# Metered background matmuls and unread filler matmuls in a four-layer attention kernel

## The chip, the core and the metric

The kernel runs on one core of a Trainium2 chip. The metric is the device time of one execution in microseconds (us); the time before is 2522.28 us, the median of six runs (2517.03 to 2527.03). The engines are named as in the profile: PE is the matrix engine (its weight loads stand apart as PEld), ACT the scalar engine, DVE the vector engine, POOL and SP the other two; SP only issues DMA transfers here. "PEclk" is the share of full speed that PE's clock was granted.

## What is computed

Four layers act on x (2048 tokens, 640 features, 32 heads of 20). Layers 0 and 2 see a sliding window of 256 keys (weights A), layers 1 and 3 see all 2048 keys (weights B).

```python
def layer(x, wqkv, wo, mask):            # mask: 0 <= i - j < 256 in layers 0 and 2, none in 1 and 3
    q, k, v = heads(layernorm(x) @ wqkv)  # 32 heads of 20
    p = softmax(where(mask, q @ k.T * 20 ** -0.5, -1e9))
    return x + join(p @ v) @ wo
x = layer(x, A...); x = layer(x, B...); x = layer(x, A...); x = layer(x, B...)
```

## The kernel before

**Units and tiles.** A unit is one layer `l`, one chunk `c` of 512 queries and one group `g` of four heads. A full-attention unit has 64 score blocks of 128 keys by 512 queries (16 key blocks for each of four heads), a windowed one has 12. The main loop (L759 to L851) takes the blocks of all units in one list, three to a *tile* (two in some early tiles), 1657 tiles in all, one a tick. In each tick it emits, in this order for PE:

1. the score matmuls of tile `t` (QK, L790) into one of two PSUM sets of three banks; heads lie in different row groups of PE and so run beside each other;
2. the exponential of the tile on ACT (L804), which reads the set and writes `pt`;
3. background work, by `pump` (called at L812);
4. the value matmuls (PV, L843) of the oldest four finished blocks, two or three tiles back, and the end of a unit when there is one.

Two PSUM sets mean that QK of tile `t` must wait for the exponential of tile `t-2`, and the exponential of tile `t` for that QK.

**Background work.** Everything that is not attention proper is a generator: layer norm and transposes (`t_ln`, L341), values (`t_v`, L382), queries and keys (`t_qk_window` L441, `t_qk_full` L455, both by `project`, L314), the normalisation of a finished unit (`t_tail`, L685) and the output projection (`t_out`, L474). Each accumulates in PSUM bank 6, the only background bank once `end_early` (L227) has given up bank 5; `drop_m` (L223) frees it for the next tick, after an evacuation by DVE (L266; by ACT in layer 0, L264).

A projection is five accumulating matmuls of 512 columns (L318). Between them the generator yields `("hold", 0.22)`, in `t_v` and `t_out` `("hold", 0.14)`; `advance` (L177) then notes the task as *held*, and `choose` (L191) gives back a held task before it looks at anything else.

```python
def choose(blocked, limit=1 << 30):
    if state["held"] is not None:
        return state["held"]
```

`pump(credit)` (L203) adds to a running credit, capped at 1.0, and advances tasks until `choose` gives none; it calls `choose(state["credit"] <= 0.0)`, and a blocked choice gives only held tasks and tails. Tasks wait in `todo` in the order of the unit that needs them first.

**Forced work.** When a unit starts, `start_unit` (L633) calls `require` (L233) for the keys, queries and values it needs. If they are not ready, `require` advances tasks there and then, ahead of the tile's QK in PE's order. For full attention, queries, keys and values go out to DRAM (`k_d`, `q_d` at L464, `v_d` at L426) and are loaded per unit by `load_unit` (vt L599, kt L606, qt L608). `load_ahead` does that early, at most one unit a tick, as soon as the unit's data are written; if it has not by the unit's start, `ensure_loaded(u, True)` does it then. A `project` sends its result to DRAM, and its task counts as ready, only when the task is advanced once more after its last matmul. Weights come by `take_w` (L292), which loads the next projection's weights ahead (L285) where it knows it, and otherwise waits four ticks.

All DMAs are issued in program order on SP's queue.

Of the kernel before, what the change touches and what calls it, by code (L numbers as in the profile page):

```python
# [31 lines left out]
def kernel(  # L32
# [10 lines left out]
    nc = tc.nc  # L43
# [37 lines left out]
    ident = big.tile([P, P], BF16, name="ident", tag="ident")  # L81
# [3 lines left out]
    masks = big.tile([P, 3, C], BF16, name="masks", tag="masks")  # L85

    ps = psp.tile([P, 8, C], F32, name="ps", tag="ps")
# [64 lines left out]
    state = {"tick": 0, "held": None, "credit": 0.0, "early": True, "act": True, "unit": 0}  # L152
# [15 lines left out]
    def push(name, gen, need):  # L168
        insort(todo, Task(name, gen, need))
# [7 lines left out]
    def advance(task):  # L177
        state["running"] = task
        try:
            kind, n = next(task.gen)  # L180
        except StopIteration:
            drop(task)
            state["held"] = None
            return 0.0
        state["held"] = task if kind == "hold" else None
        if kind == "wait":
            task.wake = state["tick"] + n
            return 0.0
        return n
# [4 lines that stand above are left out]
        for t in tails:  # L194
            if t.wake <= state["tick"]:
                return t
        if not blocked:
            for t in todo:
                if t.wake <= state["tick"] and (t.need <= limit or t.holds):
                    return t  # L200
        return None

    def pump(credit):  # L203
        state["credit"] = min(state["credit"] + credit, 1.0)
        while True:
            t = choose(state["credit"] <= 0.0)
            if t is None:
                break
            state["credit"] -= advance(t)


    mfree = {5: (0, 0), 6: (0, 1)}
# [291 lines left out]
    def push_layer(l, c):  # L504

        need = [first_use(l, c, g) for g in range(G)]
        push(("ln", l, c), t_ln(l, c), need[0])
        if l == 1:
            push(("v", l, c, 0), t_v(l, c, (0,)), need[0])
            push(("v", l, c, 1), t_v(l, c, (1,)), need[4])  # L510
        else:
            push(("v", l, c), t_v(l, c, (0, 1)), need[0])
        for g in range(G):
            key = ("qk", l, c, g)
            if l % 2:
                push_proj(key, l, 1, g, t_qk_full(key, l, c, g), need[g])
            else:
                push_proj(
                    key, l, 0, g, t_qk_window(key, l, c, g), need[g], first=(l == 0 and c == 0)
                )  # L520


    class Unit:
        def __init__(self, l, c, g, part=None):
# [58 lines left out]
    index = {(u.l, u.c, u.g, u.part): n for n, u in enumerate(units)}  # L583
# [143 lines left out]
    def t_stats0(c):  # L727
        for i in range(4):
            stats(0, c, i)
            yield ("pe", 0.1)  # L730
        ready.add(("x", 0, c))
# [12 lines left out]
    with tc.manual_schedule():  # L744
        push("stats", t_stats0(0), 0)
        push_layer(0, 0)
        require(("xnT", 0, 0))
        other_constants()
        require(("qk", 0, 0, 0))

        def narrow(u):
            return u.l == 0 or (u.l, u.part) == (1, "a")

        banks = [b for u in units for b in u.banks]
        tiles = []
        n = 0
        while n < len(banks):
            size = 2 if len(tiles) % 2 and narrow(banks[n][0]) else 3
            tiles.append(banks[n : n + size])  # L759
            n += size  # L760

        started = set()
        pts = deque()
        pushed = set()
        for t in range(len(tiles) + 8):
            state["tick"] += 1
            n_b = 0
            if t < len(tiles):
                cur = tiles[t]
                n_b = len(cur)  # L770
                for b in cur:
                    u = b[0]
                    if id(u) not in started:
                        started.add(id(u))
                        if u.l == 0 and u.g == 0 and u.c + 1 < NC and u.c not in pushed:
                            pushed.add(u.c)
                            push(("stats", u.c + 1), t_stats0(u.c + 1), index[0, u.c + 1, 0, None])
                            push_layer(0, u.c + 1)
                            if u.c == 0:
                                push("prep_b", t_prep_b(), index[0, 1, G - 1, None])  # L780
                        state["unit"] = index[u.l, u.c, u.g, u.part]
                        state["act"] = u.l == 0
                        if state["early"] and not narrow(u):
                            end_early()
                        start_unit(u)
                sp = ps[:, 0:3, :] if t % 2 == 0 else ps[:, 3:6, :]
                for n in range(2):
                    for i, (u, j, m, b0, subs, first, last, end) in enumerate(cur):
                        for kc, q0, qn, col in subs[n : n + 1]:
                            nc.tensor.matmul(  # L790
                                sp[:, i, col * P : (col + qn) * P],
                                lhsT=u.k(kc, j), rhs=u.q(j, q0, qn), start=True, stop=True,
                            )
                for b in cur:
                    if b[-1]:
                        s_emitted(b[0])
                pt = ptp.tile([P, 3, C], BF16, name="pt", tag="pt")
                i = 0
                while i < n_b:
                    b0 = cur[i][3]  # L800
                    k = i
                    while k < n_b and cur[k][3] == b0:
                        k += 1
                    nc.scalar.activation(  # L804
                        out=pt[:, i:k, b0 * P :], in_=sp[:, i:k, b0 * P :],
                        func=ACT.Exp, scale=SCALE,
                    )
                    i = k
                for i, b in enumerate(cur):
                    pts.append((t, pt, i, b))  # L810
                load_ahead()
                pump(1.2 if cur[0][0].l == 0 else 0.6)  # L812
            else:
                pump(2.0)

            if 0 < t <= len(tiles):
                cur_, pt_ = masked
                i = 0
                while i < len(cur_):
                    m, b0 = cur_[i][2:4]  # L820
                    k = i
                    while k < len(cur_) and cur_[k][2] == m:
                        k += 1
                    if m is not None:
                        mv_ = masks[:, m, b0 * P :].unsqueeze(1).to_broadcast(
                            (P, k - i, C - b0 * P)
                        )
                        nc.vector.tensor_tensor(  # L828
                            out=pt_[:, i:k, b0 * P :], in0=pt_[:, i:k, b0 * P :], in1=mv_,
                            op=ALU.mult,  # L830
                        )
                    i = k
            if n_b:
                masked = (cur, pt)

            if len(pts) >= 4 and pts[3][0] <= t - (3 if pts[0][3][0].windowed else 2):
                group = [pts.popleft() for _ in range(4)]
                u, subs, end = group[0][3][0], group[0][3][4], group[3][3][7]
                first, last = group[0][3][5:7]
                for n, (kc, q0, qn, col) in enumerate(subs):  # L840
                    for _, pt, i, b in group:
                        j = b[1]
                        nc.tensor.matmul(  # L843
                            op[32 * j : 32 * j + VW, q0 * P : (q0 + qn) * P],
                            lhsT=u.v(kc, j), rhs=pt[:, i, col * P : (col + qn) * P],
                            start=(first and n == 0), stop=(last and n == len(subs) - 1),
                            skip_group_check=u.windowed,
                        )
                if end:
                    pv_emitted(u)  # L850
                    finish_unit(u)  # L851
        while tails or todo:
            state["tick"] += 1
            pump(5.0)


# [28 lines left out]
```

The softmax here doesn't subtract the row's maximum and nothing guards it: scores larger than these inputs give would overflow.

## Time and profile before

| | |
|---|---|
| median of six runs | 2522.28 us (2517.03 to 2527.03) |
| the profiled execution | 2518.07 us, its span 2516.4 us |
| mean granted PE clock | 0.739 |
| busy in the span | PE 2065.5, PEld 729.9, DVE 852.6, ACT 2264.0, POOL 48.2 us |
| L804 exponential, ACT | 1688 instructions, 2197.9 us busy |
| L790 QK of full attention, PE | 4096, 711.7 us busy |
| L843 PV of full attention, PE | 4096, 533.4 us busy |
| L318 projections, PE | 1280, 365.1 us busy |

The profile is one execution. "Busy" for PE is the union of matmuls whose ends are modelled. A group of instructions is given with its line, its engine, its operands and the idle time of the engine just ahead of it, with what ended it. In the timeline the columns are start, duration, engine, line, operation and count; a bracket at the end of a row is the engine's idle time before it and what released it.

### The profile page before, as it was taken

How to read it: one execution, taken by the hardware profiler on the slowest of the kernel's cores; microseconds unless marked ns; L12 is line 12 of the kernel's file. 1: busy time of each engine (PE TensorE's matmuls, PEld its weight loads, DVE VectorE, ACT ScalarE, POOL GpSimd, SP SyncE). 2: the span in 40 equal slices, each digit the busy share in tenths (PEclk: the TensorE clock that was granted, in tenths of full speed). 3: DMA queues.
4: the chain of work that ended last, by engine and by line, in shares of the span. 5: the costliest groups of instructions: out<-in, count | busy, mean ns of one | idle time of the engine just before them, and what ended most of it. 6: DMA issues, size and time to landing. Idle time of an engine off the chain costs nothing.

```text
span 2516.4 us, 37514 instructions
## 1 busy us (share of the span) xinstructions
PE 2065.5 (82%) x15424; PEld 729.9 (29%) x15424; DVE 852.6 (34%) x1925; ACT 2264.0 (90%) x1831; POOL 48.2 (2%) x113
## 2 busy tenths in 40 slices
PE   6889987887878888878887888888877787778777
PEld 3334432222322233223332233223322222222222
DVE  6686843321324343424343433643200010001001
ACT  6778856889998999999999988999999999999995
POOL 2000000000000000000000000000000000000000
PEclk9899989885866699757996589968755565556555
DMA  4212133332201043101221033104211010011000
GB/s 164 70 59 63 46 98 105 111 106 69 67 28 43 27 102 103 37 31 42 91 94 43 1 84 94 65 20 116 78 36 48 32 43 32 33 46 46 32 17 11
DMA packets 92892, 153.03 MB, mean 61 GB/s; under 512 B 8880, under 2 KB 59056, under 8 KB 92720
## 3 DMA queue, kind: packets, MB, share of 16 engines
q1 hardware_dynamic: 92720, 150.64, 19.1%
q8 instruction: 120, 1.97, 0.3%
q14 instruction: 52, 0.43, 0.1%
HBM read 120.46 MB, written 30.15 MB: 60 GB/s over the span
## 4 chain that ended last, share of the span: by engine, by line
ACT 47%; PE 29%; issue 13%; DVE 8%; DMA 2%; SPq 0%; ACTq 0%; POOL 0%; DVEq 0%
ACT pt L804 46%; PE ps L318 10%; PE ps L790 6%; PE ps L843 4%; PE ps L482 4%; PE ps L405 4%; DVE pt L828 2%; DMA wqk<-wqk_d 1%; DVE oT L668 1%; PE ps L369 1%; DVE st L266 1%; DVE qa L266 1%; DMA qt<-q_d 1%; DVE x_sb L490 1%; PE ps L714 0%
## 5 line engine op out<-in xcount | busy, mean ns | idle before, releaser
L804 ACT ACTIVATE pt<-ps 128x1536 bf16<-128x1536 f32 (+1 forms) x1688 | 2197.9, 1536 | 185.7 <-PE ps L790 168.8
L790 PE MATMUL ps<-qt,kt 32*128 32x512 bf16 x4096 | 711.7, 502 | 303.6 <-ACT pt L804 270.2
L843 PE MATMUL ps<-pt,vt 128*21 128x512 bf16 x4096 | 533.4, 507 | 5.5 <-DVE oT L668 4.3
L790 PEld LDWEIGHTS <-kt 32*128 32x128 bf16 x4096 | 204.2, 95 | 771.6 <-issue 738.6
L318 PE MATMUL ps<-xnT,wqk 128*128 128x512 bf16 x1280 | 365.1, 422 | 22.6 <-DMA wqk<-wqk_d 8.1
L828 DVE TENSOR_TENSOR pt<-pt,masks 128x1024 bf16<-128x1024 bf16 (+5 forms) x403 | 240.0, 625 | 215.7 <-ACT pt L804 215.4
L668 DVE CAST oT<-ps 128x512 bf16<-128x512 f32 x117 | 80.3, 686 | 505.5 <-PE ps L843 505.1
L843 PEld LDWEIGHTS <-vt 128*21 128x21 bf16 x4096 | 105.9, 91 | 330.4 <-issue 325.9
L482 PE MATMUL ps<-wop,on 128*128 128x320 bf16 x1024 | 177.3, 321 | 10.5 <-DVE x_sb L490 5.3
L318 PEld LDWEIGHTS <-wqk 128*128 128x128 bf16 x1280 | 116.7, 104 | 193.9 <-issue 105.0
L790 PE MATMUL ps<-qa,ka 32*128 32x384 bf16 (+2 forms) x1408 | 135.6, 324 | 31.0 <-ACT pt L804 28.6
L266 DVE CAST st<-ps 128x512 bf16<-128x512 f32 x119 | 82.3, 692 | 213.7 <-PE ps L318 212.4
L490 DVE TENSOR_TENSOR x_sb<-x_sb,ps 128x320 bf16<-128x320 bf16 x128 | 61.9, 484 | 184.6 <-PE ps L482 182.1
L482 PEld LDWEIGHTS <-on 128*128 128x128 bf16 x1024 | 97.3, 103 | 77.3 <-issue 37.8
L405 PE MATMUL ps<-wv,xnT 128*128 128x320 bf16 x640 | 112.1, 313 | 7.0 <-DVE vs L266 2.1
L718 DVE TENSOR_TENSOR on<-oT,ps 128x512 bf16<-128x512 bf16 x128 | 87.5, 684 | 86.9 <-PE ps L714 85.5
L843 PE MATMUL ps<-pt,va 128*21 128x384 bf16 (+2 forms) x1408 | 89.1, 322 | 18.3 <-DVE oT L668 17.7
L695 DVE RECIPROCAL rz<-ps 128x16 f32<-128x16 f32 x128 | 32.8, 256 | 156.2 <-PE ps L690 147.2
L790 PEld LDWEIGHTS <-ka 32*128 32x128 bf16 x1408 | 39.4, 96 | 118.4 <-issue 112.8
L405 PEld LDWEIGHTS <-xnT 128*128 128x128 bf16 x640 | 58.0, 100 | 49.5 <-issue 29.3
L714 PE MATMUL ps<-rT,spread 32*128 32x128 bf16 x512 | 63.7, 258 | 2.2 <-DVE rT L707 1.3
L369 PE MATMUL ps<-ident,xn 128*128 128x128 bf16 x320 | 35.5, 257 | 25.6 <-DVE xn L360 22.7
(50 smaller groups left out, 646.2 us busy)
## 6 DMA issues: line engine op xcount, KB each, us to landing
wqk<-wqk_d SPq DMA_DIRECT2D x120, 320.0 KB
kt<-k_d SPq DMA_DIRECT2D x53, 512.0 KB
vt<-v_d SPq DMA_DIRECT2D x53, 336.0 KB
qt<-q_d SPq DMA_DIRECT2D x75, 128.0 KB
k_d<-st SPq DMA_DIRECT2D x64, 128.0 KB
q_d<-st SPq DMA_DIRECT2D x64, 128.0 KB
v_d<-vs SPq DMA_DIRECT2D x16, 336.0 KB
wqk_d<-wqk SPq DMA_DIRECT2D x16, 320.0 KB
```

Source lines behind the costliest of these rows:

```text
L266: nc.vector.tensor_copy(out=out_, in_=in_)
L318: nc.tensor.matmul(pq, lhsT=wt[:, n, dc, :], rhs=xt[:, dc, :], start=(dc == 0), stop=(dc == KD - 1),)
L405: nc.tensor.matmul(pv, lhsT=xt[:, dc, i * P : (i + 1) * P], rhs=wv_sb[l % 2][:, dc, h * HD : (h + 1) * HD], start=(dc == 0), stop=(dc == K ...
L482: nc.tensor.matmul(yp, lhsT=on[:, g, qb * P : (qb + 1) * P], rhs=wop[:, g, i * HD : (i + 1) * HD], start=(g == 0), stop=(g == G - 1),)
L490: nc.vector.tensor_tensor(out=xv, in0=xv, in1=yp, op=ALU.add)
L668: nc.vector.tensor_copy(out=oT[:], in_=op)
L714: nc.tensor.matmul(zb[:, qb * P : (qb + 1) * P], lhsT=spread4[:, qb, :], rhs=rT[:], start=True, stop=True,)
L718: nc.vector.tensor_tensor(out=on[:, g, :], in0=oT[:], in1=zb, op=ALU.mult)
L790: nc.tensor.matmul(sp[:, i, col * P : (col + qn) * P], lhsT=u.k(kc, j), rhs=u.q(j, q0, qn), start=True, stop=True,)
L804: nc.scalar.activation(out=pt[:, i:k, b0 * P :], in_=sp[:, i:k, b0 * P :], func=ACT.Exp, scale=SCALE,)
L828: nc.vector.tensor_tensor(out=pt_[:, i:k, b0 * P :], in0=pt_[:, i:k, b0 * P :], in1=mv_, op=ALU.mult,)
L843: nc.tensor.matmul(op[32 * j : 32 * j + VW, q0 * P : (q0 + qn) * P], lhsT=u.v(kc, j), rhs=pt[:, i, col * P : (col + qn) * P], start=(first ...
```

## The change

`pump` takes its cap as a second argument. In layer 0 it stays 1.2 a tick with cap 1.0. In later layers a tick adds 0.56 instead of 0.6, and the cap is 0.6 instead of 1.0. After it, up to the start of unit (3, 1, 0), a new `keep_clock` emits matmuls of 512 columns into the free background bank, from two constant tiles; nothing reads them. It does so while no task is held, the credit is over 0.2 and the bank is free in this tick, and takes 0.22 of credit for each. The calls in the last eight ticks and in the closing loop get caps of 2.0 and 5.0.

```diff
-    def pump(credit):
-        state["credit"] = min(state["credit"] + credit, 1.0)
+    def pump(credit, most):
+        state["credit"] = min(state["credit"] + credit, most)
...
+    def keep_clock():
+
+        while state["held"] is None and state["credit"] > 0.2:
+            b = min(mfree, key=mfree.get)
+            if mfree[b][0] > state["tick"]:
+                return
+            nc.tensor.matmul(
+                ps[:, b, :], lhsT=ident[:], rhs=masks[:, 0, :], start=True, stop=True
+            )
+            state["credit"] -= 0.22
...
-                pump(1.2 if cur[0][0].l == 0 else 0.6)
+                if cur[0][0].l == 0:
+                    pump(1.2, 1.0)
+                else:
+                    pump(0.56, 0.6)
+                    if state["unit"] < index[3, 1, 0, None]:
+                        keep_clock()
             else:
-                pump(2.0)
+                pump(2.0, 2.0)
...
-            pump(5.0)
+            pump(5.0, 5.0)
```

## The prediction

> **What bounds the kernel now.** I read first the shares of the page, then stretches by stage, then the idle time of ACT, then the timeline around it. ACT is busy for 90% of the span. By stage it is the bound, but not always full:
>
> ```profile
> 500.00:1800.00 1300.00, 1088.70 (x8341) 388.60 (x8341) 482.94 (x1048) 1207.33 (x911) 14.56 (x40) 0.77 0.21 64
> ...
> 1900.00:2000.00 100.00, 77.68 (x476) 20.45 (x472) 6.60 (x18) 100.00 (x76) 0.00 (x0) 0.50 0.09 31
> ```
>
> The columns are window, length, busy us of PE, PEld, DVE, ACT and POOL, PEclk, DMA share, GB/s. In 1900 to 2000 there is no background work, PE runs at half clock, and ACT is full: half clock is enough for attention alone. From 500 to 1800 ACT is idle for 1300 - 1207.33 = 92.7 us. Over the span the exponential (L804) waits 168.8 us for QK, and that time is what the change can win. What such a wait looks like:
>
> ```profile
> 712.50 3.14 ACT L804 ACTIVATE pt<-ps 128x1152 bf16<-128x1152 f32 x5
> ...
> 714.38 2.31 PE L318 MATMUL ps<-xnT,wqk 128*128 128x512 bf16 x5
> 716.62 0.61 PE L843 MATMUL ps<-pt,va 128*21 128x384 bf16 x8
> ...
> 717.16 0.61 PE L790 MATMUL ps<-qa,ka 32*128 32x384 bf16 x6
> ...
> 717.88 2.47 ACT L804 ACTIVATE pt<-ps 128x1536 bf16<-128x1536 f32 x2 [2.25 <-PE ps L790]
> ```
>
> A projection, five matmuls in one piece, takes 2.24 us (714.38 to 716.62) at half clock after a quiet stretch, QK stands behind it, and ACT idles 2.25 us. At full clock the same piece lasts 1.25 us (first row of the next fence), and single pieces in every second tile cost nothing: 895 to 945 us has ACT busy 48.89 of 50 at PEclk 1.00. There is a second kind of wait, forced work at a unit's start:
>
> ```profile
> 1565.58 1.25 PE L318 MATMUL ps<-xnT,wqk 128*128 128x512 bf16 x5 [1.19 <-DMA wqk<-wqk_d]
> ...
> 1567.61 1.24 PE L318 MATMUL ps<-xnT,wqk 128*128 128x512 bf16 x5 [0.78 <-DVE qa L266]
> ...
> 1570.06 4.13 ACT L804 ACTIVATE pt<-ps 128x1536 bf16<-128x1536 f32 x3 [4.95 <-PE ps L790]
> ```
>
> ```profile
> 420.03 0.32 SPq L464 DMA_DIRECT2D q_d<-st  x1
> ...
> 421.36 0.43 SPq L608 DMA_DIRECT2D qt<-q_d  x1
> ...
> 423.60 0.61 PE L790 MATMUL ps<-qt,kt 32*128 32x512 bf16 x3 [4.33 <-DMA qt<-q_d]
> ...
> 424.34 1.45 ACT L804 ACTIVATE pt<-ps 128x1536 bf16<-128x1536 f32 x1 [4.43 <-PE ps L790]
> ```
>
> The first shows two forced projections, 2.03 us apart because the one background bank must be evacuated between them. The second shows a unit whose queries are stored and loaded back at its start: ACT idles 4.43 us. With two forced projections ahead of the same chain (432.95) the gap is 8.00 us, with one (1490.98) it is 6.13, and where the last projection lies two tiles back (449.63) it is 2.61.
>
> **What the diff does to the order.** I compared the order of PE's instructions in the two programs, tile by tile.
>
> *Metering does not split a projection.* The five matmuls of an accumulation are held, and a held task is advanced whatever the credit. So pieces of 2.24 us stay; what the new numbers change is how often a piece comes: 0.56 instead of 0.6 a tile, and no more than 0.6 saved up. Two adjacent pieces after "155" become one tile apart in the next pair. Background falls behind by up to four projections where it has a due time.
>
> *Fillers.* 444 are added, two each in 222 tiles without other background. 195 of these tiles lie in 17 stretches of 3 to 18 tiles, nearly all in the second half of a chunk of layer 1; layer 3 after 1807 us is nearly as before.
>
> *Forced work grows.* At the start of unit (1, 0, 0, b), 420 us, two projections where none was; at (3, 0, 0, a), 1490 us, two for one; at (2, 3, 0), 1565 us, six for two. And units (1, 0, 4), (1, 0, 5), (1, 0, 6), which were loaded 4, 6 and 7 tiles ahead, are now loaded at their start: the last projection stands one, one and two tiles before it, fillers in the tiles ahead of that.
>
> **Costs.**
> 1. (1, 0, 0, b): the gap of 4.43 becomes one like 432.95, 8.00: +3.6.
> 2. (1, 0, 4) to (1, 0, 6): two gaps like 4.43, one like 2.61, 11.5 together. After such a stall the clock has dropped, and the next piece has cost 1.04 to 1.36 (443.74, 459.91): three times 1.2 is 3.6. The double pieces at 524.91 and 555.92 (2.93 and 3.14 of gap) now lie inside these stalls and go. 11.5 + 3.6 - 6.1 = +9.0.
> 3. (3, 0, 0, a): 8.00 - 6.13 = +1.9.
> 4. (2, 3, 0): four more projections at 2.03: +8.1. Their weights took 4.08 us to land at 1561.45, the length of two projections, so I add nothing for them.
> 5. Fillers. No row has one, so bounds: nothing, where PE is at full clock (QK to next start 0.33, two at 0.216, PV about 0.3: 1.1 of ACT's 1.36 us a tile); at half clock, QK 0.54 to the next start, two at 0.45, PV 0.54 in three tiles of four: 1.84 us against 1.36. The rise takes about 5 us (the pieces from 2035.96 on: 2.25, 1.89, then 1.25). In 5 us PE does 2.7 tiles and ACT could do 3.7; one tile late, less the 0.75 by which QK is ahead, leaves about 0.4 (1.2 if nothing is ahead). 17 stretches: +6.8, bounds 0 and 20.
>
> The fillers wait for nothing new: the bank's evacuation was emitted at least a tick earlier, and DVE's 0.69 us copy is over. The next user of the bank is PE itself. DMA and POOL get no new work. The end, from the last exponential, has the same PE order.
>
> **Gains.** I listed each gap of the timeline over 0.4 us with the order of the changed program ahead of it.
> - A. First piece after a filler stretch: 715.63, 756.90, 799.57, 1047.53, 1096.37, 1338.93, 1381.69: 2.25 + 1.66 + 2.19 + 1.41 + 1.34 + 1.41 + 1.41 = 11.7. At full clock one piece costs about nothing: 11.0.
> - B. The piece after that, behind three tiles of a unit's tail (722.21, the rest at 756.90, 806.08, 1089.54, 1345.83, 1388.58): 2.06 + 2.58 + 2.33 + 1.1 + 2.07 + 1.22 = 11.4. Two adjacent pieces cost 1.29 even at full clock (1054.42), and the three tail tiles hold little PE work. At full clock a tile without background has about 0.4 of 1.36 us of matmul streaming, and after the pieces from 2035.96 on such tiles lose the clock within some 5 us: PEclk is 1.00 in 2056 to 2061 and 0.51 in 2061 to 2071. I take it to drop in half of the cases: 5.0.
> - C. Pieces behind tails with one filler tile, and transposes after the stretches (1150.78, 1440.95, 1474.56, 1704.16 and the like, 13.2 in all): 2.7.
> - D. The split doubles, nine of about 0.3; and the 5.14 gap at 383.14, a weight load that now has a tile more: 1.3 less. 3.8 (bounds 2 and 6).
>
> **Sum.** Costs 3.6 + 9.0 + 1.9 + 8.1 + 6.8 = 29.4; gains 11.0 + 5.0 + 2.7 + 3.8 = 22.5; net +6.9. Against the profiled execution's 2518.07 that is 2525; the median of the runs stands 4.2 above it, so 2529. Layer 0 and the last 700 us stay.
>
> [...]
>
> **Rivals.**
> - *Faster: the clock holds through the tail tiles.* Then B gives 7.5 (each down to its value at full clock, 1.29 or 0), C 7.2, and few stretches start at half clock (2 instead of 6.8): gains 11.7 + 7.5 + 7.2 + 3.8 = 30.2, costs 24.6, net -5.6: 2517, and 2510 if the three late loads cost half, as in the next case. It decides from the point where the tiles between stretches keep PEclk at 1.0. For: 2046 to 2056, clock 1.00 with light tiles among the pieces. Against: the drop at 2061.
> - *Same: the late loads cost half.* SP runs ahead of the other engines and may issue them sooner than their place says. Then cost 2 is 5.8 + 2.4 - 6.1 = 2.1, net 0.0, 2522. Against: they stand behind the store of a projection that is itself late, as at 420.03.
> - *Much slower: fillers start cold and stay a burden.* 17 times 1.2 is 20, B and C give 0: costs 42.6, gains 14.8, net +28: 2550; with half of that, 2540.
> - *It does not meter.* This is no rival but in the sum: if I misread it and pieces were split into two or three, a cold piece would stall ACT by under 1 us where it did by 1.4, worth some 15 us more: 2514.
>
> **Chances.** Forecast (2520 to 2537) 0.45; much slower 0.18; same 0.17; faster 0.20. 0.2% is 5 us, about what a measurement of this kernel can tell from no change: 2517.2 to 2527.3. The forecast's own spread lies with two thirds of it above that. Slower 0.30 + 0.18 + 0.04 = 0.52, same 0.26, faster 0.22. The range, 2511 to 2543, leaves out the far ends of the faster and the much slower case.
>
> **What would show it.** Pieces of L318 still in fives; 444 new matmuls, PEclk near 1.0 in filler stretches with ACT near full (bare tiles in the last 700 us stay at 0.50); the gaps of A gone; gaps of L804 of about 8 near 420, 4 to 5 near 490, 525 and 555, 8 near 1490 and 13 near 1565. If the gaps at 490 to 555 are missing, cost 2 is wrong; if filler stretches show ACT idle at their starts, cost 5 is larger.

## The result and the profile after

The changed kernel takes 2537.48 us, the median of 20 runs (2527.51 to 2543.60), against 2522.22 us for the kernel before in 45 runs. The ratio is 1.0058 with a 95% interval of 1.0049 to 1.0067: 15.3 us slower. Its profiled execution took 2533.38 us (span 2531.7), 15.3 us more than the one of before, though the mean granted clock rose from 0.739 to 0.80. The exponential is now L815, QK L801, PV L859, the filler L528.

From the page after, the slices of PE's clock and groups by line:

```profile
PEclk9999998889998898887999789889855565556556
...
L815 ACT ACTIVATE pt<-ps 128x1536 bf16<-128x1536 f32 (+1 forms) x1688 | 2197.2, 1528 | 205.6 <-PE ps L801 180.9
...
L528 PE MATMUL ps<-masks,ident 128*128 128x512 bf16 x444 | 149.5, 422 | 0.2 <-DVE on L729 0.2
```

The exponential's row before was:

```profile
L804 ACT ACTIVATE pt<-ps 128x1536 bf16<-128x1536 f32 (+1 forms) x1688 | 2197.9, 1536 | 185.7 <-PE ps L790 168.8
```

ACT does the same work (2197.2 us of exponentials, 2197.9 before) and waits more: 180.9 us for QK where it was 168.8. PE's clock is at 7 tenths or more in the first 29 of the 40 slices, and at 5 and 6 in the last 11, where no filler is. The projections are a little faster (355.3 us, 365.1 before). The windows of the two stages, columns as above:

```profile
500.00:1800.00 1300.00, 1119.64 (x8688) 402.56 (x8688) 478.88 (x1037) 1190.66 (x899) 14.62 (x40) 0.88 0.21 63
1900.00:2000.00 100.00, 78.31 (x485) 21.18 (x484) 8.80 (x24) 100.00 (x75) 0.00 (x0) 0.50 0.12 41
```

In 500 to 1800 PE's clock rose from 0.77 to 0.88 and ACT fell from 1207.33 to 1190.66 us of work. The untouched end is as it was, clock 0.50 with ACT full.

To place the loss, take the same two exponentials in both programs and compare the time between them (stretches named by their times before; difference in us, profiled executions):

| stretch | before | after | metering alone (e1) | 0.60 with fillers (e5) | best (e12) |
|---|---|---|---|---|---|
| 28-318, layer 0 | 290.4 | -3.7 | +2.2 | -3.8 | +0.3 |
| 318-418 | 100.1 | -3.1 | -2.4 | -0.4 | +5.5 |
| 418-445, start of (1,0,0,b) | 26.6 | +2.1 | +1.6 | +1.6 | -15.3 |
| 445-489 | 44.0 | -2.4 | 0.0 | -1.5 | -2.7 |
| 489-570, units (1,0,4) to (1,0,6) | 80.9 | **+13.9** | **+19.3** | -5.7 | -4.8 |
| 570-1486 | 916.2 | +1.6 | -1.2 | -1.9 | -3.2 |
| 1486-1507, start of (3,0,0,a) | 21.2 | +1.9 | +2.2 | +0.9 | +0.7 |
| 1507-1558 | 50.4 | -0.6 | -0.6 | -1.2 | -0.1 |
| 1558-1577, start of (2,3,0) | 19.2 | **+6.7** | **+6.7** | +0.8 | -5.2 |
| 1577-1803 | 226.2 | +0.8 | +1.8 | +2.3 | +1.0 |
| 1803-2490 | 686.8 | -0.5 | -1.1 | -1.2 | +0.1 |
| start and end | | -1.4 | +2.0 | +1.1 | -0.8 |

Four short stretches, where a unit's work comes due, hold 24.6 us of loss (2.1 + 13.9 + 1.9 + 6.7). Everything else together is 9.3 us better, of which 3.7 are in layer 0, where PE's order is the same in the two programs.

A late load in the timeline after, at the start of unit (1, 0, 4):

```profile
485.08 0.32 SPq L464 DMA_DIRECT2D q_d<-st  x1
485.49 0.38 SPq L610 DMA_DIRECT2D vt<-v_d  x1
485.97 0.40 SPq L617 DMA_DIRECT2D kt<-k_d  x1
486.42 0.42 SPq L619 DMA_DIRECT2D qt<-q_d  x1
...
490.53 0.61 PE L801 MATMUL ps<-qt,kt 32*128 32x512 bf16 x2 [5.57 <-DMA qt<-q_d]
...
491.24 1.45 ACT L815 ACTIVATE pt<-ps 128x1536 bf16<-128x1536 f32 x1 [6.54 <-PE ps L801]
```

The queries go out at 485.08, all three loads stand behind that store, and QK can start 5.45 us after it. ACT waits 6.54 us. The next two units show the same: 6.30 at 521.85, then 4.94 and 1.88 at 560.35 and 566.74.

Forced projections in the timeline after, at the start of unit (2, 3, 0):

```profile
1573.74 1.24 PE L318 MATMUL ps<-xnT,wqk 128*128 128x512 bf16 x5 [0.26 <-DVE va L266]
...
1575.76 1.24 PE L318 MATMUL ps<-xnT,wqk 128*128 128x512 bf16 x5 [0.78 <-DVE st L266]
...
1583.84 1.24 PE L318 MATMUL ps<-xnT,wqk 128*128 128x512 bf16 x5 [0.78 <-DVE qa L266]
...
1586.29 1.45 ACT L815 ACTIVATE pt<-ps 128x1536 bf16<-128x1536 f32 x1 [11.87 <-PE ps L801]
```

Six of them, 2.02 us from one to the next, the last five waiting 0.78 us each for DVE to empty the one bank, and ACT stands still for 11.87 us where it was 4.95.

And what the fillers do well: the timeline after at the first piece that followed a quiet stretch (2.25 us of gap before the change):

```profile
715.34 8.45 ACT L815 ACTIVATE pt<-ps 128x1536 bf16<-128x1536 f32 x9
...
721.21 0.61 PE L528 MATMUL ps<-masks,ident 128*128 128x512 bf16 x2
...
722.32 1.25 PE L318 MATMUL ps<-xnT,wqk 128*128 128x512 bf16 x5
...
724.33 4.33 ACT L815 ACTIVATE pt<-ps 128x1536 bf16<-128x1536 f32 x6 [0.54 <-PE ps L801]
```

The piece takes 1.25 us instead of 2.24. ACT runs nine exponentials without a gap, and the gap behind the piece is 0.54 us.

### The profile page after: what moved, and what is told of

Same layout as the page of the kernel before. It is cut to its first block, busy times and chain, and to the rows that moved or that the text cites. A ratio compares the mean times of both kernels' runs of the same rounds, so it can differ in the third digit from the quotient of the medians.

```text
span 2531.7 us, 38403 instructions
## 1 busy us (share of the span) xinstructions
PE 2102.4 (83%) x15868; PEld 747.6 (30%) x15868; DVE 852.2 (34%) x1925; ACT 2263.1 (89%) x1831; POOL 48.3 (2%) x113
## 4 chain that ended last, share of the span: by engine, by line
ACT 46%; PE 27%; issue 15%; DVE 9%; DMA 2%; SPq 0%; ACTq 0%; POOL 0%; DVEq 0%
ACT pt L815 45%; PE ps L318 9%; PE ps L801 6%; PE ps L859 4%; DVE pt L844 3%; PE ps L405 3%; PE ps L482 3%; PE ps L528 1%; DMA qt<-q_d 1%; DVE oT L679 1%; PE ps L369 1%; DVE st L266 1%; DVE on L729 1%; DVE xn L360 0%; DVE qa L266 0%
## 5 line engine op out<-in xcount | busy, mean ns | idle before, releaser
L815 ACT ACTIVATE pt<-ps 128x1536 bf16<-128x1536 f32 (+1 forms) x1688 | 2197.2, 1528 | 205.6 <-PE ps L801 180.9
L801 PE MATMUL ps<-qt,kt 32*128 32x512 bf16 x4096 | 681.7, 481 | 287.6 <-ACT pt L815 229.0
L859 PE MATMUL ps<-pt,vt 128*21 128x512 bf16 x4096 | 506.4, 481 | 5.7 <-DVE oT L679 4.0
L801 PEld LDWEIGHTS <-kt 32*128 32x128 bf16 x4096 | 201.6, 94 | 738.0 <-issue 681.9
L318 PE MATMUL ps<-xnT,wqk 128*128 128x512 bf16 x1280 | 355.3, 413 | 26.5 <-DVE st L266 6.9
L859 PEld LDWEIGHTS <-vt 128*21 128x21 bf16 x4096 | 105.1, 91 | 342.7 <-issue 338.1
L318 PEld LDWEIGHTS <-wqk 128*128 128x128 bf16 x1280 | 115.7, 102 | 192.2 <-issue 102.5
L528 PE MATMUL ps<-masks,ident 128*128 128x512 bf16 x444 | 149.5, 422 | 0.2 <-DVE on L729 0.2
L801 PE MATMUL ps<-qa,ka 32*128 32x384 bf16 (+2 forms) x1408 | 115.6, 279 | 25.3 <-ACT pt L815 20.3
L859 PE MATMUL ps<-pt,va 128*21 128x384 bf16 (+2 forms) x1408 | 81.1, 296 | 16.3 <-DVE oT L679 15.9
L801 PEld LDWEIGHTS <-ka 32*128 32x128 bf16 x1408 | 39.9, 92 | 97.0 <-issue 88.7
```

The source lines that it names most:

```text
L318: nc.tensor.matmul(pq, lhsT=wt[:, n, dc, :], rhs=xt[:, dc, :], start=(dc == 0), stop=(dc == KD - 1),)
L528: nc.tensor.matmul(ps[:, b, :], lhsT=ident[:], rhs=masks[:, 0, :], start=True, stop=True)
L801: nc.tensor.matmul(sp[:, i, col * P : (col + qn) * P], lhsT=u.k(kc, j), rhs=u.q(j, q0, qn), start=True, stop=True,)
L815: nc.scalar.activation(out=pt[:, i:k, b0 * P :], in_=sp[:, i:k, b0 * P :], func=ACT.Exp, scale=SCALE,)
L859: nc.tensor.matmul(op[32 * j : 32 * j + VW, q0 * P : (q0 + qn) * P], lhsT=u.v(kc, j), rhs=pt[:, i, col * P : (col + qn) * P], start=(first ...
```

## The experiments

Medians stand beside the kernel before on the same chip (2520.99 us for e1 to e4, 2523.57 for e5 and e7 to e9, 2522.70 for e10 to e13); the ratio is to that, with its 95% interval. Where nothing else is said, a diff is against the changed kernel.

### e1: metering without fillers

```diff
                     pump(0.56, 0.6)
-                    if state["unit"] < index[3, 1, 0, None]:
-                        keep_clock()
```

> The changed kernel without its 444 fillers: 0.56 credit a tile, cap 0.6, the same order of background work as the changed kernel. Theory (late work carries the loss): in the two traces the changed kernel loses about 25 us at six places where a unit starts (3 near 420, 14 between 485 and 572, 2 near 1498, 7 near 1574), and all these stay; expected 2535 to 2542, 13 to 20 over before. Rival (the fillers carry the loss): the metering alone is near neutral, 2520 to 2528. As this case's prediction had its terms: costs 1 to 4 are 22.6, gain D 3.8, together +19.

Measured: 2547.48 us, 1.0104 (1.0081 to 1.0127), +26.5 us, beyond the expected range. The clock is 0.740, as before. The metering is the loss, and in the changed kernel the fillers give some 11 us back (1.0104 to 1.0058).

### e2: fillers without metering

```diff
-        while state["held"] is None and state["credit"] > 0.2:
+        for _ in range(2):
+            if state["held"] is not None or state["credit"] <= 0.2:
+                return
...
-            state["credit"] -= 0.22
...
-                    pump(0.56, 0.6)
+                    pump(0.6, 1.0)
```

The fillers take no credit here, two in a tile, 522 in all, and background work comes as in the kernel before.

> The kernel before with two fillers laid into each tile that has no other background work and credit over 0.2 (522 in 261 tiles); they take no credit, so rate (0.6), cap (1.0), background order and unit starts are those of before. The prediction's terms: gains A to C 18.7 less 6.8 for starts of stretches, -12: 2510. Theory after the two traces (fillers pay back what they cost: tiles of a stretch that begins at half clock lost 1.0 to 1.9 us each against before, and even a single filler tile at half clock 0.7 to 0.9): 2517 to 2526, no change that can be told. Rival (fillers alone carry the loss): 2532 or more.

Measured: 2515.06 us, 0.9981 (0.9967 to 0.9995), clock 0.808. Fillers alone are worth about 5 us. That is between my prediction's terms (2510) and the theory that they cost as much as they bring. In the profiles the gain lies at 489 to 570 (6.8 us); 570 to 1486, which has most of the gaps of A to C, is 3.2 us worse than before.

### e3: one filler in place of two

The edit is that of e2 with `range(1)`.

> As the kernel before with fillers, but one filler a tile instead of two (261). At half clock a tile then needs on PE 0.54 (QK) + 0.45 + 0.54 in three tiles of four, about 1.4 us against ACT's 1.36, so starting at half clock should cost nothing. If one filler is enough to raise and hold the clock, the gains of about 12 to 18 come free: 2506 to 2513. If it raises the clock but doesn't hold it, a part of them: 2513 to 2519. If it does neither, 2520 to 2524, as before, with PEclk in the stretches at 0.5.

Measured: 2537.75 us, 1.0070 (1.0047 to 1.0093), slower than before and than any theory had it. The loss is in 570 to 1486: +24.2 us there, against +3.2 for e2. The timeline of e3 in a stretch of filler tiles shows why:

```profile
604.88 0.61 PE L802 MATMUL ps<-qt,kt 32*128 32x512 bf16 x3
...
605.42 0.61 PE L530 MATMUL ps<-masks,ident 128*128 128x512 bf16 x1
...
605.96 0.61 PE L860 MATMUL ps<-pt,vt 128*21 128x512 bf16 x4
...
606.50 0.61 PE L802 MATMUL ps<-qt,kt 32*128 32x512 bf16 x3
```

A tile takes 0.54 for QK, 0.54 for the filler and 0.54 for PV: 1.62 us at half clock, where ACT needs about 1.36 (at 604.52 three exponentials in a row take 4.15 us, where a single one takes 1.45: 1.35 from one to the next). The windows of e3:

```profile
597.00:632.00 35.00, 33.33 (x181) 8.40 (x183) 3.46 (x9) 32.31 (x25) 0.00 (x0) 0.54 0.08 29
603.40:606.80 3.40, 3.40 (x19) 0.62 (x15) 0.00 (x0) 3.23 (x3) 0.00 (x0) 0.50 0.00 0
```

The same window in e2, then in the kernel before:

```profile
597.00:632.00 35.00, 31.85 (x213) 10.89 (x215) 4.66 (x12) 32.36 (x25) 0.00 (x0) 0.85 0.09 29
```

```profile
597.00:632.00 35.00, 28.08 (x172) 8.27 (x171) 4.20 (x12) 34.38 (x27) 0.00 (x0) 0.51 0.10 34
```

One filler makes PE the bound (busy all 3.40 us of the second window) and the clock stays at 0.50. Two fillers cost as much at first, 32.36 us of ACT's work in the window, but raise the clock to 0.85, and e2 is near the kernel before over the whole of 570 to 1486. So here one filler a tile was worse than none (1.0070), and two were not (0.9981).

### e4: fillers up to the end

e2 without the limit at unit (3, 1, 0): 1316 fillers, most of them in the last 700 us, where ACT was full at half clock.

> As the kernel before with two fillers a tile that take no credit, but without the limit at the last layer's second chunk: 1316 fillers in 658 tiles, 397 of these tiles in the last 700 us, where ACT is full without them and there is little for a raised clock to win. It measures what fillers cost by themselves. Theory (each start of a stretch at half clock costs 1.0 to 1.9 us): some 24 units end there, each with tail tiles that let the clock drop, and each is followed by a stretch, some by short ones too: 24 to 50 us over the kernel with fillers up to that chunk alone. Prediction's size (0.4 a start): about 10 over it. If fillers cost nothing: equal to it.

Measured: 2522.14 us, 1.0010 (0.9995 to 1.0025), 7 us above e2. This was to measure what a filler stretch costs where it can gain nothing. A window of e4:

```profile
1900.00:2000.00 100.00, 83.18 (x582) 26.38 (x592) 8.79 (x24) 97.91 (x74) 0.00 (x0) 0.93 0.12 41
```

The clock is 0.93 instead of 0.50, and ACT loses 2.09 us of 100. In the profiles the loss over 1803 to 2490 is 16.0 us in 24 filler stretches, 0.67 each, and 3.0 come back after the last exponential; by the medians it is 7 us, 0.3 each. The theory of a lasting burden expected 24 to 50 and falls by both; the size of the prediction, about 10, lies between the two.

### e5 and e11: the old rate with the new cap, with and without fillers

```diff
-                    pump(0.56, 0.6)
+                    pump(0.6, 0.6)
```

e11 is e5 without the call of `keep_clock`.

> The changed kernel with 0.60 credit a tile instead of 0.56, cap 0.6 and fillers kept. In the order of its instructions the unit at 420 us has no forced projection, the three units from 485 to 572 us are loaded ahead again (the first by three tiles), the unit at 1498 has one forced projection and that at 1574 three instead of six. Theory (the rate, through late units, is the loss): these places took 25 us in the changed kernel; 2 should be left at the last one, so 2514 to 2519, faster than before. Rival (the cap is the loss): still 2530 or more.

> The changed kernel with rate 0.60 and without fillers, so that of the change only the cap of 0.6 stays. With fillers this rate gave 2513.7, 10 under before. If fillers give that (they gave 10 between the metering alone and the changed kernel, 6 on the schedule of before): 2521 to 2527. If the cap gives it (two adjacent pieces are moved apart, about 4 by the traces): 2515 to 2520.

Measured: e5 2513.65 us, 0.9956 (0.9940 to 0.9972); e11 2517.44 us, 0.9981 (0.9969 to 0.9993). Without fillers, 0.60 against 0.56 is 0.9981 against 1.0104, 31 us; with them 0.9956 against 1.0058, 26 us. So **at a cap of 0.6 the 0.04 of rate is the loss**, and the rival "the cap is the loss" falls. The cap of 0.6 alone (e11) is worth about 5 us, as its second theory had it. Group L790 before, then L801 by lines with QK's waits, after and then in e5:

```profile
L790 PE MATMUL ps<-qt,kt 32*128 32x512 bf16 x4096 | 711.7, 502 | 303.6 <-ACT pt L804 270.2 <-DMA qt<-q_d 21.3
```

```profile
L801 PE MATMUL ps<-qt,kt 32*128 32x512 bf16 x4096 | 681.7, 481 | 287.6 <-ACT pt L815 229.0 <-DMA qt<-q_d 38.9
```

```profile
L801 PE MATMUL ps<-qt,kt 32*128 32x512 bf16 x4096 | 676.4, 477 | 269.1 <-ACT pt L815 227.0 <-DMA qt<-q_d 23.0
```

QK's wait for a unit's queries is 39 us at 0.56, with or without fillers (39.3 in e1), and 23 at 0.60 (21.3 before). In 489 to 570 e5 is 19.6 us better than the changed kernel (+13.9 to -5.7): the first of the three units is loaded three tiles ahead again. At (2, 3, 0) three projections are forced instead of six (5.9 us).

### e7: the new rate with the old cap

```diff
-                    pump(0.56, 0.6)
+                    pump(0.56, 1.0)
```

> The changed kernel with the cap back at 1.0, rate 0.56 and fillers kept (633, as the larger credit pays for up to four a tile at the start of a stretch). The units from 485 to 572 us are loaded one to three tiles ahead instead of at their start, forced work at 420 and 1498 stays that of the changed kernel, at 1574 it is four projections. Theory: about 10 to 14 of the 14 us between 485 and 572 come back, and 4 of 7 at 1574: 2519 to 2525. Rival (loads of one to three tiles ahead are still late, a load took about 3.6 us from the end of its projection): 2528 to 2533.

Measured: 2523.50 us, 1.0000 (0.9983 to 1.0016). At a rate of 0.56 the lower cap costs 0.58%, 14.6 us. Background again falls behind, but less: the three units are loaded one to three tiles ahead, with gaps of 4.07 us at the first and 4.83 at the third, and four projections are forced at (2, 3, 0). At 0.60 the lower cap costs nothing (e11 against before: 0.9981).

The total is in the theory's range, but not for the theory's reason. Of the 13.9 us at 489 to 570 only 7.0 come back, and of the 6.7 at (2, 3, 0) 0.9. The larger part lies in 570 to 1486, which is 11.1 us better than before and 12.7 better than the changed kernel: there are 528 fillers in it instead of 368, its mean clock is 0.93 instead of 0.88, and ACT is idle for 44.8 us instead of 55.1. So the larger cap gave credit to late work and, more so, to fillers. The rate of 0.56 with the old cap and without fillers was not run.

### e8 and e13: a higher rate, with and without fillers

```diff
-                    pump(0.56, 0.6)
+                    pump(0.7, 0.6)
```

e8 has this and the free fillers of e2. e13 is the kernel before with 0.7 for 0.6 and nothing else.

> The kernel before with two fillers a tile that take no credit, rate 0.70 and cap 0.6: the opposite of the change in rate. No unit after 360 us has forced projections; only the units at 445 and 1490 us are loaded at their start or two tiles ahead. The kernel before lost about 4.4 at 420, 8.0 at 433, 6 at 1491 and 5 at 1565. Theory (late units are the larger loss, and fillers pay a little): 2498 to 2508. Rival (pieces of projections now stand in two tiles of three, and PE becomes the bound there; a piece, QK and PV take 1.08 + 0.33 + 0.3 of ACT's 1.36 us): 2515 to 2525.

> The kernel before with 0.70 credit a tile instead of 0.6, nothing else. Units as in the run with rate 0.70 and fillers (2512.0). Theory (the rate sets when units are ready, fillers pay 6 to 10 apart from it): 2516 to 2522. Rival (fillers give nothing once units are in time): 2508 to 2514.

Measured: e8 2512.00 us, 0.9951 (0.9933 to 0.9969), between the two theories; e13 2525.90 us, 1.0018 (1.0007 to 1.0028), above both of its theories. With 0.7 no projection is forced after 360 us, and in both the stretch 418-445 gains 15.3 us and 1558-1577 gains 5.2. But 570 to 1486, where nothing is due soon, loses 8.6 (e8) and 14.3 us (e13). Pieces come closer together there, with a mean clock of 0.90 in e8 and 0.73 in e13; that this is the cause is argued, not shown. In these runs the higher rate paid only near a due time.

### e9 and e10: pieces that are really split

The prediction priced the case that a projection is split between tiles at some 15 us less. e9 blocks a held task too when the credit is spent; e10 does so from layer 1 on. Both have rate 0.7, cap 1.0 and no fillers, so e13 is e10's control. The diff is that of e10, against the kernel before; in e9 the line is `return None if blocked else state["held"]`.

```diff
     if state["held"] is not None:
-        return state["held"]
+        return None if blocked and not state["act"] else state["held"]
...
-                pump(1.2 if cur[0][0].l == 0 else 0.6)
+                pump(1.2 if cur[0][0].l == 0 else 0.7)
```

> Metering as the change's words have it: a held task is blocked too when the credit is spent, so a projection is split over tiles, two to four matmuls in each; no fillers, rate 0.70 so that units are not much later than before (forced work at 445 and 1565 us, one unit loaded two tiles ahead), cap 1.0. Theory by the prediction's last case: a piece of two or three at half clock stalls ACT by under 1 us instead of 1.4 to 2.2, worth up to 15 us: 2505 to 2515. Rival (the bank is held for two tiles, so tails and other tasks wait and pile up; each switch between kinds of matmul costs about 0.1 us at half clock): 2522 to 2535.

> The split projection again, but from layer 1 on alone: the earlier run split in layer 0 too and lost 50 us there, which mixes two questions. Rate 0.70, cap 1.0, no fillers; its control is the kernel before with rate 0.70, which runs beside it. Theory (a held bank keeps tails and other tasks waiting for a tile more, units come late): over its control by 10 to 30. Prediction's last case (smaller pieces stall ACT less): 5 to 15 under its control.

Measured: e9 2600.86 us, 1.0305 (1.0283 to 1.0326). It lost 49.9 us in layer 0, which I had not meant to touch; as a test of splitting it tells nothing. e10: 2521.14 us, 0.9994 (0.9984 to 1.0004), 5 to 6 us under e13. My theory that splitting costs 10 to 30 us falls; the net is about a third of the prediction's price. The runs do not show its reason, that cold pieces stall ACT less: 570 to 1486, where most of them lie, is 16.3 us worse than before in e10 and 14.3 in e13. In 1558 to 1577, where e10 forces projections and e13 none, e10 loses 9.3 us against e13.

### e12: the higher rate only where units are due

```diff
+        quiet = 0
...
-                    pump(0.56, 0.6)
-                    if state["unit"] < index[3, 1, 0, None]:
+                    due = state["unit"] < index[1, 1, 0, None]
+                    due = due or index[1, 3, 5, None] <= state["unit"] < index[2, 3, 1, None]
+                    was = min(state["credit"] + (0.7 if due else 0.6), 0.6)
+                    pump(0.7 if due else 0.6, 0.6)
+                    quiet = quiet + 1 if state["credit"] == was else 0
+                    if quiet >= 2 and state["unit"] < index[3, 1, 0, None]:
                         keep_clock()
```

Here the free fillers of e2 start only in the second tile in a row without background work.

> Cap 0.6, two fillers a tile that take no credit and only from the second tile in a row without other work; rate 0.70 in the units where layer 1 starts and where layer 3 starts, 0.60 elsewhere. No unit after 360 us has forced projections, two are loaded at or close to their start. Theory: the late units of before (about 15 us saved at 420 to 440, 5 at 1565 in the run with rate 0.70) and the fillers' 6 to 10 add up: 2498 to 2506, faster than both kernels. Rival (PE's extra pieces there eat it, as in that run, which gave 2512): 2510 to 2516.

Measured: **2493.56 us, 0.9884 (0.9868 to 0.9899)**, 29 us under the kernel before, some 44 under the changed one, and below its theory's range. Its windows, and QK by lines (L803, its exponential is L817):

```profile
500.00:1800.00 1300.00, 1120.36 (x8778) 410.51 (x8880) 481.71 (x1052) 1221.25 (x920) 14.61 (x40) 0.88 0.21 63
```

```profile
L803 PE MATMUL ps<-qt,kt 32*128 32x512 bf16 x4096 | 679.9, 480 | 248.4 <-ACT pt L817 219.7 <-DMA qt<-q_d 10.1
```

PE's clock in the window is the 0.88 of the changed kernel, and PE is as busy (1120.36 against 1119.64). ACT does 1221.25 us of work instead of 1190.66. The clock is the same, so it is not what differs; little is late: QK waits 10.1 us for queries instead of 38.9. In the timeline, around the start of unit (1, 0, 0, b):

```profile
411.50 6.20 ACT L817 ACTIVATE pt<-ps 128x1536 bf16<-128x1536 f32 x5 [0.49 <-PE ps L803]
...
418.08 5.77 ACT L817 ACTIVATE pt<-ps 128x1024 bf16<-128x1024 f32 x5 [0.38 <-PE ps L803]
```

The gaps ahead of these rows are 0.49 and 0.38 us, in the stretch that had gaps of 4.43 and 8.00 us. e12 changes two things against e8: the rate is 0.60 where nothing is due, and fillers start a tile later. In 570 to 1486 e12 is 11.8 us better than e8; no run parts the two.

## Why the prediction was right, and where its terms were off

The sign and the mechanism were right: slower by late work at units' starts, with fillers that win part of it back. The size was too small: the net was +6.9 and is +15.3, and 2537.48 us lies just above the forecast's 2520 to 2537, inside the range up to 2543. Nor was the order of the costs right: cost 5 is as large as cost 2. By its own steps:

- **Pieces stay whole:** right. L318 comes in rows of five, 1280 in all.
- **Cost 1, (1, 0, 0, b):** foretold +3.6 with a gap of 8.00; the gap is 7.59 and the stretch +2.1. About right.
- **Cost 2, units (1, 0, 4) to (1, 0, 6): mis-sized.** Foretold +9.0, measured +13.9, and +19.3 without fillers. The step that failed is "two gaps like 4.43, one like 2.61". The row at 423.60 that I took the gap from belongs to a part unit, which loads 4 of the 16 key blocks. A full unit loads four times the keys and values ahead of its queries, and QK could start 4.11 us after the issue of qt (486.42 to 490.53) instead of 2.24 (421.36 to 423.60). The nearer row was 1490.98, a unit of 12 key blocks with a gap of 6.13, less the one forced projection that it holds; there it was 3.40 us, in the trace before:

```profile
1493.04 0.43 SPq L608 DMA_DIRECT2D qt<-q_d  x1
...
1496.44 0.61 PE L790 MATMUL ps<-qt,kt 32*128 32x512 bf16 x4 [5.18 <-DMA qt<-q_d]
```

So it is 2.24 us with 4 key blocks ahead of the queries, 3.40 with 12 and 4.11 with 16. The rival "the late loads cost half" falls.
- **Cost 3, (3, 0, 0, a):** +1.9 foretold, +1.9 measured, gap 8.86. Right.
- **Cost 4, (2, 3, 0):** +8.1 foretold, +6.7 measured. Right in kind: 2.02 us a projection, and PE waited for DVE, not for weights, before each of the six pieces.
- **Cost 5, the fillers' starts: mis-sized, within its bounds.** Foretold 6.8 for 17 stretches of 0.4, measured about 14 in 36. Of the 17 long stretches eight start at half clock, 8.7 us together. Three of them, where the clock rose 3.3 to 3.5 us after the first filler, cost 0.4 to 0.6 each; five, where it rose after 5.4 to 6.1, cost 1.1 to 1.9. The short stretches, single tiles mostly at 0.3 to 0.8, I had left out; they cost some 5 us together. A long start in the timeline after:

```profile
822.56 0.61 PE L801 MATMUL ps<-qt,kt 32*128 32x512 bf16 x3
...
823.11 1.03 PE L528 MATMUL ps<-masks,ident 128*128 128x512 bf16 x2
...
824.07 0.61 PE L801 MATMUL ps<-qt,kt 32*128 32x512 bf16 x3
...
826.12 0.61 PE L801 MATMUL ps<-qt,kt 32*128 32x512 bf16 x3
```

A tile without PV takes 1.51 us here (822.56 to 824.07), one with PV 2.05 (824.07 to 826.12). With PV in three tiles of four that is 1.91, where I had put 1.84: two fillers hold PE for 0.96 us, not 0.90. The clock rose 5.5 us after the first filler, near the 5 of the prediction, with PE busy all the time until then:

```profile
823.10:828.60 5.50, 5.50 (x26) 0.90 (x23) 0.00 (x0) 4.57 (x4) 0.00 (x0) 0.50 0.00 0
828.70:845.80 17.10, 15.42 (x115) 4.85 (x116) 2.43 (x4) 16.92 (x15) 0.00 (x0) 1.00 0.06 18
```

So neither the tile nor the rise was far off. What failed is the deduction "less the 0.75 by which QK is ahead": this start cost 1.3 us, near the bound "1.2 if nothing is ahead".

- **Gain A, first piece after a filler stretch:** 11.0 foretold; the seven gaps shrank from 11.7 us to 1.3. Right.
- **Gain B, the piece behind a unit's tail: wrong.** 5.0 foretold on "I take it to drop in half of the cases". Of the six places one (1089.54) went from 1.1 us to nothing; the other five went from 10.3 us to 10.6. In four of these five the piece still runs at half clock, so the rival "the clock holds through the tail tiles" falls too.
- **Gain C:** 2.7 foretold. The four places that it names went from 7.7 us to 4.9, but e1, which has no fillers, has 5.8 there. So most of this is not the fillers' gain; the other places are not listed, and the term as a whole stays open.
- **Gain D:** 3.8 foretold. In e1, which has no fillers, the stretches between the four (318-418, 445-489, 570-1486, 1507-1558) are together 4.2 us better. About right.

Metering alone was foretold at 22.6 - 3.8 = +18.8 and is +26.5 (e1). The fillers were foretold at 11.0 + 5.0 + 2.7 - 6.8 = 11.9 of gain; they bring about 11 by the medians, but not where I put it. In 570 to 1486, which has most of the gaps of A to C, after is 2.8 us worse than e1: about what A wins, the starts cost. What can be placed lies at 445 to 570 (7.8 us), between the late loads, where the mean clock in 489 to 570 is 0.85 instead of 0.81. The other differences of the two profiles lie in layer 0 and at the start and end, which have no fillers. So the right sum of the fillers is luck.

The rival "much slower" had the fillers' side nearer: starts of 20 us, and nothing for B and C (measured about 14, 0.8 and little). With half of its terms it gave 2540.

The terms' errors add up to more than the miss of 8.4 us. Against them stand gains that I had not listed, such as 2.4 us in 445 to 489, and 3.7 us in layer 0 that the change does not explain. I did not split the remainder further.

The gains A to C rest on fillers that raise the clock and hold it. That this happens here is shown by the 10.4 us of A, and by the granted clock in 1900 to 2000: 0.50 without fillers (after, PE busy 78.31 us of 100), 0.93 with them (e4, PE busy 83.18). That tiles without other work lose it is shown by the fall at 2061 in the trace before:

```profile
2056.00:2061.00 5.00, 2.87 (x29) 1.04 (x29) 0.87 (x2) 5.00 (x5) 0.00 (x0) 1.00 0.09 33
2061.00:2071.00 10.00, 8.02 (x53) 2.39 (x52) 1.82 (x6) 10.00 (x9) 0.00 (x0) 0.51 0.29 102
```

The clock goes from 1.00 to 0.51, and PE's longest idle time from 2054 to 2061 is 0.95 us.

## What to carry to other kernels

A rate for background work is set by its due times: at a cap of 0.6, 7% less of it cost 31 us, most of it at two places, and saved little elsewhere, so look first for what becomes late, then raise the rate there alone. Price a late load by a row with the same bytes ahead of it (here QK could start 2.24, 3.40 and 4.11 us after the issue, with 4, 12 and 16 key blocks ahead), not by the nearest row in time. Fillers that hold PE's clock must be enough to raise it (in 597 to 632 one a tile gave a mean clock of 0.54, two gave 0.85, none 0.51), and belong only where a piece at half clock would otherwise hold up the bound engine.

## What the hardware showed that I had not expected

- **The granted clock stayed at half while PE had no idle time.** In e3 PE is busy all 3.40 us of the window from 603.40 to 606.80, at a clock of 0.50. Over 597 to 632 PE is busier with one filler a tile (33.33 of 35 us, e3) than with two (31.85, e2), and the mean clock is 0.54 against 0.85; before, it is 28.08 us and 0.51. So in these windows PE's busy share does not tell which has the higher clock. What the clock follows is not shown.
- **Matmuls of different kinds stood further apart on PE than two of the same kind.** At half clock QK, one filler and PV follow each other at 0.54 us (e3), while after two fillers in a row the next matmul starts 0.96 us after the first (823.11 to 824.07): a second of the same kind adds 0.42. By the difference of the two I estimate the change of kind at about 0.12 us.
- **The same order of instructions differs by some us between executions.** Layer 0 is untouched in all kernels but e9, and its 290.4 us came out 3.8 us shorter to 2.2 longer. Profiles alone don't carry a verdict of that size; the medians must.
